# Holding back the third relu and the third square of a visit behind the next product

## The chip, the cores and the metric

The kernel runs on one core of a Trainium2 chip. The metric is the device time of that core in microseconds (us). Runs are told as fast or slow; here a run is slow when it took over 1.5% longer than the fastest of the same kernel. Times are medians of several runs. A ratio is the mean time of one kernel's fast runs over that of the other's fast runs of the same rounds, so it is not quite the ratio of the medians quoted beside it. The engines are called as in the profile: PE is TensorE, PEld its weight loads, ACT ScalarE, DVE VectorE, POOL GpSimd, SP the engine that issues most DMAs.

## The reference

```python
scores = (1 / sqrt(64)) * q @ k.T        # 8 x 12 heads, 448 x 448 each
attn   = maximum(scores, 0) ** 2 / 448
x      = (attn @ v)                      # laid out as 3584 tokens x 768
h      = x @ w_in                        # 768 -> 2048
g      = h * 1 / (1 + exp(-1.702 * h))   # sigmoid form of GELU
out    = g @ w_out                       # 2048 -> 768
```

Inputs and output are float32; the kernel multiplies in float16.

## The kernel before

The 96 heads are handled as 24 units of four heads; a unit has seven score tiles (`s`) and one product with v (`v`). The tokens go through the two weight matrices in eight groups of 384 or 512. The kernel places every instruction by hand: a scheduler of its own emits *visits* (the next three attention items) between *products*, which are `m1` (first matrix, 6 matmuls into `ht`, then a GELU) and `m2` (second matrix, 16 matmuls into `op`, then an evacuation to `osb`). On each engine instructions run in the order of emission.

```python
ps_s = ...tile_pool(name="ps_s", bufs=3, space=PSUM)   # scores and products with v, two banks each
ps_m = ...tile_pool(name="ps_m", bufs=2, space=PSUM)   # ht, op and PE transposes, one bank each

def relu2(u, j, sc):
    ...                                                 # units 3 to 5, j == 3: relu on VectorE
        nc.scalar.activation(out=rl, in_=sc[:, :, 0:S], func=AF.Relu)
    nc.vector.tensor_tensor(out=at, in0=rl, in1=rl, op=ALU.mult)
    return at

def visit(n):
    new = items[pos[0]:pos[0] + n]
    ...
    for t, u, j in new:                                 # first all matmuls of the visit
        if t == "s":
            made.append(scores(u, j))
        else:
            ...                                         # av_mm of all seven ats of the unit
    for (t, u, j), sc in zip(new, made):                # then what reads them
        if t == "s":
            ats[u, j] = relu2(u, j, sc)
        else:
            xt_evac(u)
            done_units[0] = u + 1

def m1(g, f):
    ht = ps_m.tile([128, 512], F32, name="ht", tag="mm")
    ...                                                 # 6 matmuls
    nc.scalar.activation(out=gf[:, 0:n], in_=ht[:, 0:n], func=AF.Gelu_apprx_sigmoid, scale=1.0 / SC)
    nc.gpsimd.tensor_scalar(out=gts[g][:, f, 0:n], in0=gf[:, 0:n], ...)

def m2(g, m, h):
    ...
        op = ps_m.tile([128, 512], F32, name="op", tag="mm")
        ...                                             # 16 matmuls
        nc.vector.tensor_scalar(out=ot[:, lo:lo + w], in0=op[:, 0:w], scalar1=1.0 / SC, ...)
    ...                                                 # store

def step_visit(n):
    visit(n)
    ...
    prefetch(u + 4, u + 2)                              # loads; casts of k (VectorE) and q (GpSimd); DMA transposes
```

A visit's three relus stand in ScalarE's queue ahead of the GELU of the product that follows, and its squares in VectorE's ahead of that product's evacuation.

Of the kernel before, what the change touches and what calls it, by code (L numbers as in the profile page):

```python
# [15 lines left out]
def kernel(  # L16
# [120 lines left out]
    def scores(u, j):  # L137
        st = units[u]
        sc = ps_s.tile([128, 2, 512], F32, name="sc", tag="sc")
        for s in range(2):  # L140
            for a in range(2):
                r = slice(64 * a, 64 * a + 64)
                c = slice(64 * s, 64 * s + 64)
                nc.tensor.matmul(  # L144
                    out=sc[c, a, 0:S],
                    lhsT=st["kT"][r, j, c],
                    rhs=st["qT"][r, :, c],
                    start=True, stop=True)
        return sc

    def relu2(u, j, sc):
        rl = rlp.tile([128, 2, S], F16, name="rl", tag="rl")
        at = atp.tile([128, 2, S], F16, name="at", tag="at")
        if NP <= u < 2 * NP and j == 3:
            nc.vector.tensor_scalar(out=rl, in0=sc[:, :, 0:S], scalar1=0.0, scalar2=None,  # L155
                                    op0=ALU.max)
# [5 lines that stand above are left out]
    def av_mm(u, j, at):  # L162
        st = units[u]
        if j == 0:
            st["av"] = ps_s.tile([128, 2, 512], F32, name="av", tag="sc")
        for s in range(2):
            for a in range(2):
                r = slice(64 * s, 64 * s + 64)
                nc.tensor.matmul(  # L169
                    out=st["av"][64 * a:64 * a + 64, s, 0:S],  # L170
                    lhsT=st["v16"][r, a, 64 * j:64 * j + 64],
                    rhs=at[r, a, :],
                    start=(j == 0), stop=(j == J - 1))
# [3 lines left out]
    def xt_evac(u):  # L177
        b, pr = divmod(u, NP)
        av = units[u]["av"]
        lo = b * J  # L180
        while lo < (b + 1) * J:
            g = max(i for i in range(NG) if gcum[i] <= lo)
            hi = min((b + 1) * J, gcum[g + 1])
            if g not in xts:
                xts[g] = xtp.tile([128, NK, 512], F16, name="xt", tag="xt")
            nc.vector.tensor_copy(  # L186
                out=xts[g][:, 2 * pr:2 * pr + 2, 64 * (lo - gcum[g]):64 * (hi - gcum[g])],
                in_=av[:, :, 64 * (lo - b * J):64 * (hi - b * J)])
            lo = hi
        units[u] = None  # L190
# [12 lines left out]
    ats = {}  # L203
    pos = [0]
    done_units = [0]

    def visit(n):
        new = items[pos[0]:pos[0] + n]
        if new and ("v", new[-1][1], 0) == new[-1] and ("s", new[-1][1], J - 1) in new:
            new.pop()  # L210
        pos[0] += len(new)
        made = []
        for t, u, j in new:
            if t == "s":
                made.append(scores(u, j))
            else:
                for jj in range(J):
                    av_mm(u, jj, ats.pop((u, jj)))
                made.append(None)
        for (t, u, j), sc in zip(new, made):  # L220
            if t == "s":
                ats[u, j] = relu2(u, j, sc)
            else:
                xt_evac(u)
                done_units[0] = u + 1


    gts = {}

    def m1(g, f):  # L230
        n = 64 * gblk[g]
        if f == 0:
            gts[g] = gtp.tile([128, NF, 512], F16, name="gt", tag="gt")
        ht = ps_m.tile([128, 512], F32, name="ht", tag="mm")
        w = win[f // WQ]
        fo = (f % WQ) * 128
        for kk in range(NK):
            nc.tensor.matmul(  # L238
                out=ht[:, 0:n], lhsT=w[:, kk, fo:fo + 128],
                rhs=xts[g][:, kk, 0:n],  # L240
                start=(kk == 0), stop=(kk == NK - 1))
        gf = gfp.tile([128, 512], F32, name="gf", tag="gf")
        nc.scalar.activation(out=gf[:, 0:n], in_=ht[:, 0:n],  # L243
                             func=AF.Gelu_apprx_sigmoid, scale=1.0 / SC)
        nc.gpsimd.tensor_scalar(out=gts[g][:, f, 0:n], in0=gf[:, 0:n],  # L245
                                scalar1=SC, scalar2=1.0, op0=ALU.mult, op1=ALU.mult)

    osb = {}

    def store(g, m, lo, hi, engs):  # L250
        for i in range(2):
            b, j = divmod(gcum[g] + 2 * m + i, J)
            r0 = b * S + j
            engs[i].dma_start(out=out[r0:r0 + 63 * J + 1:J, lo:hi],
                              in_=osb[g, m][64 * i:64 * i + 64, lo:hi])

    def m2(g, m, h):
        if h == 0:
            osb[g, m] = osp.tile([128, DM], F32, name="osb", tag="osb")
        ot = osb[g, m]  # L260
        last = g == NG - 1 and m == gblk[g] // 2 - 1
        for part in range(2 if last and h == 1 else 1):
            w = NOUT // 2 if last and h == 1 else NOUT
            op = ps_m.tile([128, 512], F32, name="op", tag="mm")
            for f in range(NF):
                nc.tensor.matmul(  # L266
                    out=op[:, 0:w],
                    lhsT=gts[g][:, f, m * 128:(m + 1) * 128],
                    rhs=wout[h][f // WO][:, f % WO, part * w:(part + 1) * w],
                    start=(f == 0), stop=(f == NF - 1))  # L270
            lo = h * NOUT + part * w
            nc.vector.tensor_scalar(out=ot[:, lo:lo + w], in0=op[:, 0:w],  # L272
                                    scalar1=1.0 / SC, scalar2=None, op0=ALU.mult)
            if last:
                store(g, m, lo, lo + w, (nc.sync, nc.scalar))
        if h == 1 and not last:
            store(g, m, 0, DM, (nc.sync, nc.sync))

    w_rows = moe_w_in.rearrange("(a kk d) f -> a d kk f", a=2, d=D)

# [31 lines left out]
    with tc.manual_schedule():  # L312
# [23 lines left out]
        while pos[0] < b0:  # L336
            visit(1)
            n += 1
            if n == 4:
                trans_pe(1, "k", 0)  # L340
                trans_pe(1, "q", 0)
                load16(4, "k")
                load16(4, "q")
                load_v(4)
                w1(2)
            if n == 11:
                trans_pe(2, "k", 0)
                trans_pe(2, "q", 0)
                load16(5, "k")
                load16(5, "q")  # L350
                load_v(5)
            if n == 19:
                trans_pe(3, "k", 0)
                trans_pe(3, "q", 0)
                w1(3)
        visit(3)


# [3 lines left out]
        for f in range(NF):  # L362
            m1(0, f)
            if f in (2, 8):
                trans_pe(4 + f // 8, "k", 0)
                trans_pe(4 + f // 8, "q", 0)
            if f in pool_work:
                pool_work[f]()
            if f % 2 == 1 or f > 12:
                visit(min(3, b1 - pos[0]))  # L370
# [19 lines left out]
        for m in range(gblk[0] // 2):  # L390
            m2(0, m, 0)
# [18 lines left out]
        for n, (it, tv) in enumerate(moe):  # L410
            if n == 0:
                prefetch(9, 7)
            if n == 2:
                prefetch(9, 8)
                acc = 2.0
            if it[0] == "m1":
                g = it[1]
                need = NP * min(B, -(-gcum[g + 1] // J))
                while done_units[0] < need:
                    step_visit(3)  # L420
                m1(*it[1:])
                acc += t1(g)
                if it[2] == NF - 1:
                    m1_done = g + 1
            else:
                m2(*it[1:])
                acc += T2
            while acc >= tv and pos[0] < len(items):

                if all(t == "s" or u // NP - 2 < m1_done for t, u, j in items[pos[0]:pos[0] + 3]):  # L430
                    step_visit(3)
                    acc -= tv
                else:
                    acc = tv - 0.01
# [30 lines left out]
```

## Time and profile before

The kernel took 413.97 us (three runs, 412.87 to 414.67). The profiled execution spans 410.5 us.

| stretch, us | what runs | PE busy | ACT busy | DVE busy |
|---|---|---|---|---|
| 0 to 60 | attention of units 0 to 5, first `ht` | 43.8 of 60 | 41.7 | 38.4 |
| 60 to 105 | first `op`, units 6 to 8 | 42.9 of 45 | 26.2 | 22.7 |
| 105 to 335 | all three kinds mixed, units 9 to 23 | 224.3 of 230 | 125.3 | 118.5 |
| from 335 | `ht` and `op` alone | 71.3 of 76 | 12.5 | 10.2 |

To read it: PE is nearly full from 60 us on, so an idle ACT or DVE costs nothing there; only a gap on PE does.

### The profile page before, as it was taken

The page shows a single profiled execution, that of the slowest core. Times are in us where ns is not written, and L with a number is a line of the kernel's source. Part 1 is how long each engine was busy: PE and PEld are TensorE (multiplying, and loading weights), DVE is VectorE, ACT ScalarE, POOL GpSimd, SP SyncE. Part 2 cuts the span into 40 slices and gives each one's busy share as a digit, 9 for nine tenths or more (in the row PEclk, how much of TensorE's full clock was granted, in tenths as well). Part 3 has the DMA queues.
Part 4 walks back from the last instruction along what each step waited for, and adds up shares of the span by engine and source line. Part 5 has one row for each costly group of instructions (what it writes and reads, how often), then busy time and mean ns, then how long its engine had stood idle before and what let it go on. Part 6 is the DMA issues. An engine that isn't in the chain of part 4 may idle for free.

```text
span 410.5 us, 7828 instructions
## 1 busy us (share of the span) xinstructions
PE 382.3 (93%) x3192; PEld 200.7 (49%) x3192; DVE 189.7 (46%) x294; ACT 205.7 (50%) x297; POOL 131.6 (32%) x200
## 2 busy tenths in 40 slices
PE   3777999999998999999999898999999999999995
PEld 2433445444444554454455454444445556455564
DVE  0995773367665464366466445546354421110121
ACT  3984770776664555456655635547645511222100
POOL 8443433453433142333233223312312211223100
PEclk9999999999999999999999999999999999999999
DMA  8999996889668654963667465845121111111123
GB/s 123 196 205 204 205 301 127 188 187 225 153 150 182 162 102 81 235 123 101 170 112 155 80 154 152 195 53 75 43 46 40 38 40 39 40 38 41 38 77 79
DMA packets 65222, 50.85 MB, mean 124 GB/s; under 512 B 35745, under 2 KB 61729, under 8 KB 65185
## 3 DMA queue, kind: packets, MB, share of 16 engines
q1 hardware_dynamic: 47792, 35.60, 35.5%
q0 software_dynamic: 17152, 14.55, 23.8%
q8 instruction: 25, 0.41, 0.4%
q10 hardware_dynamic: 240, 0.20, 0.2%
q14 instruction: 13, 0.10, 0.1%
HBM read 45.61 MB, written 11.01 MB: 138 GB/s over the span
## 4 chain that ended last, share of the span: by engine, by line
PE 76%; ACT 9%; DVE 8%; issue 4%; DMA 2%; POOL 0%; ACTq 0%; DVEq 0%; POOLq 0%
PE op L266 35%; PE ht L238 27%; ACT rl L158 7%; PE av L169 7%; PE sc L144 6%; DVE at L159 4%; ACT gf L243 2%; DMA q<-in_q_dram 1%; DVE rl L155 1%; DMA qT<-q 1%; DVE xt L186 1%; DVE kT L134 1%; DVE qT L134 0%; DVE osb L272 0%; POOL gt L245 0%
## 5 line engine op out<-in xcount | busy, mean ns | idle before, releaser
L158 ACT ACTIVATE rl<-sc 128x896 f16<-128x896 f32 x165 | 140.9, 920 | 58.9 <-PE sc L144 58.9
L238 PE MATMUL ht<-xt,win 128*128 128x384 f16 (+1 forms) x768 | 158.8, 353 | 4.6 <-DVE kT L134 2.1
L266 PE MATMUL op<-wout,gt 128*128 128x384 f16 (+1 forms) x912 | 153.2, 323 | 4.1 <-ACT gf L243 4.1
L245 POOL TENSOR_SCALAR gt<-gf 128x384 f16<-128x384 f32 (+1 forms) x128 | 78.4, 612 | 239.3 <-ACT gf L243 237.5
L159 DVE TENSOR_TENSOR at<-rl 128x896 f16<-128x896 f16 x168 | 113.3, 687 | 78.4 <-ACT rl L158 78.2
L243 ACT ACTIVATE gf<-ht 128x384 f32<-128x384 f32 (+1 forms) x128 | 69.1, 553 | 113.5 <-PE ht L238 100.1
L266 PEld LDWEIGHTS <-gt 128*128 128x128 f16 x912 | 88.0, 98 | 66.1 <-issue 8.8
L238 PEld LDWEIGHTS <-win 128*128 128x128 f16 x768 | 71.0, 98 | 82.7 <-issue 22.9
L272 DVE TENSOR_SCALAR osb<-op 128x384 f32<-128x384 f32 (+1 forms) x57 | 31.2, 548 | 121.2 <-PE op L266 121.2
L144 PE MATMUL sc<-qT,kT 64*64 64x448 f16 x672 | 47.5, 363 | 6.9 <-DVE qT L134 3.6
L169 PE MATMUL av<-at,v 64*64 64x448 f16 x672 | 36.5, 351 | 1.9 <-ACT rl L158 1.5
L144 PEld LDWEIGHTS <-kT 64*64 64x64 f16 x672 | 16.7, 106 | 32.2 <-issue 20.7
L186 DVE CAST xt<-av 128x768 f16<-128x768 f32 (+2 forms) x36 | 26.8, 772 | 8.8 <-PE av L169 8.8
L169 PEld LDWEIGHTS <-v 64*64 64x64 f16 x672 | 19.5, 107 | 15.7 <-issue 6.4
L88 POOL DMA_DIRECT2D v<-in_v_dram x24 | 17.9, 747 | 3.9 <-DMA win<-in_moe_w_in_dram 2.2
L101 POOL CAST q<-qst 128x896 f16<-128x896 f32 x18 | 16.9, 941 | 0.3
L101 DVE CAST k<-kst 128x896 f16<-128x896 f32 x18 | 14.0, 784 | 0.0
L127 PE MATMUL tr<-ident,k 128*64 128x128 f16 x84 | 4.2, 253 | 5.2 <-DMA k<-in_k_dram 5.2
L134 DVE COPY qT<-tr 128x896 f16<-128x896 f16 (+1 forms) x6 | 3.4, 570 | 7.5 <-ACT qT L132 7.5
L127 PEld LDWEIGHTS <-k 128*64 128x64 f16 x84 | 3.1, 128 | 6.9 <-DMA k<-in_k_dram 5.2
L283 POOL DMA_DIRECT2D win<-in_moe_w_in_dram x8 | 5.4, 682 | 3.0 <-DMA k<-in_k_dram 1.7
L127 PE MATMUL tr<-ident,q 128*64 128x128 f16 x84 | 4.2, 251 | 1.3 <-ACT gf L243 0.7
(17 smaller groups left out, 26.3 us busy)
## 6 DMA issues: line engine op xcount, KB each, us to landing
out_dram<-osb SPq DMA_DIRECT2D x54, 192.0 KB, 2.7
kst<-in_k_dram SPq DMA_DIRECT2D x18, 448.0 KB, 5.0
qst<-in_q_dram SPq DMA_DIRECT2D x18, 448.0 KB, 5.7
v<-in_v_dram POOLq DMA_DIRECT2D x24, 224.0 KB, 4.6
win<-in_moe_w_in_dram POOLq DMA_DIRECT2D x8, 384.0 KB, 11.4
wout<-in_moe_w_out_dram POOLq DMA_DIRECT2D x4, 768.0 KB, 12.0
k<-in_k_dram POOLq DMA_DIRECT2D x6, 224.0 KB, 8.8
q<-in_q_dram POOLq DMA_DIRECT2D x6, 224.0 KB, 8.7
```

What stands on the lines that cost most here:

```text
L88: nc.gpsimd.dma_start(out=x, in_=quad(v, b, pr))
L101: eng.tensor_copy(out=o, in_=i)
L144: nc.tensor.matmul(out=sc[c, a, 0:S], lhsT=st["kT"][r, j, c], rhs=st["qT"][r, :, c], start=True, stop=True)
L158: nc.scalar.activation(out=rl, in_=sc[:, :, 0:S], func=AF.Relu)
L159: nc.vector.tensor_tensor(out=at, in0=rl, in1=rl, op=ALU.mult)
L169: nc.tensor.matmul(out=st["av"][64 * a:64 * a + 64, s, 0:S], lhsT=st["v16"][r, a, 64 * j:64 * j + 64], rhs=at[r, a, :], start=(j == 0), st ...
L186: nc.vector.tensor_copy(out=xts[g][:, 2 * pr:2 * pr + 2, 64 * (lo - gcum[g]):64 * (hi - gcum[g])], in_=av[:, :, 64 * (lo - b * J):64 * (hi ...
L238: nc.tensor.matmul(out=ht[:, 0:n], lhsT=w[:, kk, fo:fo + 128], rhs=xts[g][:, kk, 0:n], start=(kk == 0), stop=(kk == NK - 1))
L243: nc.scalar.activation(out=gf[:, 0:n], in_=ht[:, 0:n], func=AF.Gelu_apprx_sigmoid, scale=1.0 / SC)
L245: nc.gpsimd.tensor_scalar(out=gts[g][:, f, 0:n], in0=gf[:, 0:n], scalar1=SC, scalar2=1.0, op0=ALU.mult, op1=ALU.mult)
L266: nc.tensor.matmul(out=op[:, 0:w], lhsT=gts[g][:, f, m * 128:(m + 1) * 128], rhs=wout[h][f // WO][:, f % WO, part * w:(part + 1) * w], sta ...
L272: nc.vector.tensor_scalar(out=ot[:, lo:lo + w], in0=op[:, 0:w], scalar1=1.0 / SC, scalar2=None, op0=ALU.mult)
```

## The change

The third relu of a visit is to let the GELU of the next product pass, so that the PSUM buffer (PSUM is where the matmuls put their results) of that product comes free sooner; and the third square is to let the evacuation of an `op` pass, for the same purpose.

```diff
+    held = []
+
+    def release():
+        while held:
+            u, j, sc = held.pop()
+            ats[u, j] = relu2(u, j, sc)
+
     def visit(n):
         ...
         pos[0] += len(new)
+        release()
         ...
-        for (t, u, j), sc in zip(new, made):
-            if t == "s":
-                ats[u, j] = relu2(u, j, sc)
-            else:
+
+        for i, ((t, u, j), sc) in enumerate(zip(new, made)):
+            if t == "v":
                 xt_evac(u)
                 done_units[0] = u + 1
+            elif i == 2:
+                held.append((u, j, sc))
+            else:
+                ats[u, j] = relu2(u, j, sc)
     def m1(g, f):
         ...                                             # after the GELU and its scaling
+        release()
     def m2(g, m, h):
         ...                                             # after the evacuation and the store
+        release()
```

## The prediction

> **What bounds the kernel now.** I began with the page: busy shares first, then the groups of instructions.
>
> ```profile
> PE 382.3 (93%) x3192; PEld 200.7 (49%) x3192; DVE 189.7 (46%) x294; ACT 205.7 (50%) x297; POOL 131.6 (32%) x200
> ...
> L158 ACT ACTIVATE rl<-sc 128x896 f16<-128x896 f32 x165 | 140.9, 920 | 58.9 <-PE sc L144 58.9
> ```
>
> TensorE (PE) is busy for 93% of the span, ScalarE (ACT) and VectorE (DVE) for about half. Matmul ends are modelled, so I measured the distance from one matmul's start to the next instead. Inside one product it is steady: 0.1625 us for 384 columns, 0.216 us for 512. A product of the first matrix (`ht`, 6 matmuls) takes 0.98 or 1.30 us, one of the second (`op`, 16 matmuls) 2.60 us, the three scores of a visit 0.69 us. From 330 us on there is no gap at all. The distances that exceed these sum to some 25 us, 13.4 us of them before 50 us, where ACT feeds the attention alone. So PE is the bound from about 30 us on, and a change to ACT and DVE order can win only the rest, about 11 us of gaps. The list of waits names who ends the gaps:
>
> ```profile
> ACT gf L243 <- PE ht L238: 100.1, 57, 8.6
> ...
> PE op L266 <- ACT gf L243: 4.1, 7, 0.6
> ```
>
> The first row is idleness of an engine that is not the bound, and costs nothing. The second is the target: seven times a product `op` waited for a GELU (`gf`). The timeline of PE, ACT and DVE around one of them:
>
> ```profile
> 111.27 0.76 PE L144 MATMUL sc<-qT,kT 64*64 64x448 f16 x12
> ...
> 111.71 2.54 ACT L158 ACTIVATE rl<-sc 128x896 f16<-128x896 f32 x3 [2.27 <-PE sc L144]
> ...
> 111.96 2.12 PE L238 MATMUL ht<-xt,win 128*128 128x384 f16 x12
> ...
> 114.11 0.89 ACT L243 ACTIVATE gf<-ht 128x384 f32<-128x384 f32 x2
> ...
> 114.67 2.76 PE L266 MATMUL op<-wout,gt 128*128 128x384 f16 x16 [0.58 <-ACT gf L243]
> ```
>
> The visit's scores start at 111.27. ACT takes the three relus from 111.71, 0.80 us apart, and reaches the GELU only at 114.11, although the first `ht` was ready long before. The next `op` reuses that `ht`'s PSUM buffer (the pool `ps_m` has two), and starts at 114.67. The 12 matmuls of the two `ht` take 12 x 0.1625 = 1.95 us, so it could have started at 111.96 + 1.95 = 113.91. The loss is 0.75 us, more than the 0.58 us printed as idle, because a modelled matmul end covers the rest. The same gap of 0.75 us stands at 113.8, 157.5, 229.0, 235.1, 247.7, 253.8 and 320.4: each is a visit of three scores, then two 384-column `ht`, then an `op`.
>
> A second kind of gap is on DVE, near 131 us:
>
> ```profile
> 131.10 0.61 DVE L101 CAST k<-kst 128x896 f16<-128x896 f32 x1
> ...
> 131.64 0.54 DVE L272 TENSOR_SCALAR osb<-op 128x384 f32<-128x384 f32 x1
> ...
> 132.23 1.14 PE L238 MATMUL ht<-xt,win 128*128 128x384 f16 x6 [1.19 <-DVE osb L272]
> ```
>
> There the visit is followed by `op` and then two `ht`; a k cast and the third square stand ahead of the evacuation of `op` (`osb`), and the second `ht` waits for it. Its loss is 1.36 us from start to start.
>
> **What the Trainium skill says.** "PSUM — Partial Sum Buffer", section "Engine vs sequencer instructions", says that the queues of ScalarE and VectorE are strict FIFO; the trace agrees, the GELU at 114.11 comes after all three relus. "ScalarE: Activation LUTs", section "What ACT_TABLE_LOAD costs", gives 186 ns + 0.833 ns per element, less about 93 ns back to back: 932 ns for 896 elements against 920 ns measured, and 839 ns spacing against 0.80 us here. "Perfetto Trace Analysis", section "Optimization Strategy", says that a repeating bubble on the engine that should be saturated can mean too few buffers; seven equal gaps at a two-buffer pool are that. "SBUF — State Buffer", section "SBUF: two separate sides", says that a VectorE operation with two SBUF inputs and a GpSimd operation lock each other out; I see one square of 2.02 us at 128.09 beside a GpSimd cast, against 0.61 us for its neighbours, which fits.
>
> **The change part by part.** No instruction is added or removed. The order of ACT changes where a product `ht` follows a visit whose third item is a score: relu, relu, GELU, relu. Where `op` follows, ACT keeps its order and DVE gets square, square, evacuation, square. Visits of fewer than three items, or whose third item is the product with v, keep theirs. The k cast issued right after a visit moves ahead of the held square.
>
> *Gains.* (1) The GELU moves up by one relu slot, 0.80 us, to 111.71 + 2 x 0.80 = 113.31. From its start to the `op` start took 114.67 - 114.11 = 0.56 us, so `op` is free at 113.87, just before 113.91. Seven gaps: 7 x 0.75 = 5.25 us. (2) Two visits followed by three 512-column `ht` (164.2 and 293.3 us) lose 0.217 us each the same way: 0.43 us. (3) Evacuations move up by one square slot, 0.53 us: the gap at 130.7 us falls by 0.53, that of 0.46 us at 299.5 us vanishes: 0.99 us together. (4) At 93.0 us scores wait 0.79 us for a DMA transpose of k, whose cast stood behind a third square; the cast moves up by about 0.8 us: 0.73 us. Sum 7.4 us.
>
> *Losses.* The held relu now waits for the `ht` and for its GELU. From the start of `ht` to the start of its GELU on a free ACT is 1.24 us (132.23 to 133.47) or, with 512 columns, 1.56 us (164.62 to 166.17); the next relu follows 0.39 or 0.48 us later and takes 0.92 us. So after a visit of three scores it ends 3.4 or 3.65 us after the first score instead of 2.97. It holds a score buffer (three in `ps_s`) until then. That is harmless where two or more products separate visits, which is nearly everywhere after 96 us; it hurts where one `ht` does:
>
> ```profile
> 76.01 0.76 PE L144 MATMUL sc<-qT,kT 64*64 64x448 f16 x12 [0.64 <-DMA qT<-q]
> ...
> 76.44 2.53 ACT L158 ACTIVATE rl<-sc 128x896 f16<-128x896 f32 x3 [0.38 <-PE sc L144]
> ...
> 76.70 1.47 PE L238 MATMUL ht<-xt,win 128*128 128x512 f16 x6
> ...
> 78.10 0.57 PE L144 MATMUL sc<-qT,kT 64*64 64x448 f16 x8
> ...
> 78.85 0.62 ACT L243 ACTIVATE gf<-ht 128x512 f32<-128x512 f32 x1
> ...
> 79.02 0.38 PE L144 MATMUL sc<-qT,kT 64*64 64x448 f16 x4 [0.35 <-ACT rl L158]
> ```
>
> The third score of the second visit waits for the relu of the third score of the first. It could start at 76.01 + 3.65 + 0.05 = 79.71 instead of 79.02: 0.69 us. A like place at 86 us costs about 0.08 us, and one at 45 us, two narrow `ht` apart, 0.16 us. At 59 to 61 us the product with v needs the square of the held relu: the GELU can begin at 59.29, the relu at 59.69, its square ends at 61.28 instead of 60.87: 0.41 us. And in the transposes of q and k on PE:
>
> ```profile
> 46.21 1.73 ACT L158 ACTIVATE rl<-sc 128x896 f16<-128x896 f32 x2
> ...
> 47.82 0.50 ACT L243 ACTIVATE gf<-ht 128x384 f32<-128x384 f32 x1
> 48.37 0.58 PE L127 MATMUL tr<-ident,q 128*64 128x128 f16 x14 [0.43 <-ACT gf L243]
> ...
> 48.76 0.61 DVE L134 COPY kT<-tr 128x896 f16<-128x896 f16 x1
> ...
> 49.43 0.81 PE L238 MATMUL ht<-xt,win 128*128 128x384 f16 x4 [0.48 <-DVE kT L134]
> ```
>
> The GELU can start at 46.28 + 1.24 = 47.52, which lets the q transpose begin 0.3 us sooner. But the held relu then runs 47.92 to 48.84, its square to 49.5, and the copy of kT stands behind that square on DVE: 49.42 to 50.03 instead of 48.76 to 49.37, and the `ht` behind it starts 0.66 us later. The twin place at 35 us is bound by a relu on DVE and stays. Sum of losses 0.16 + 0.66 + 0.41 + 0.69 + 0.08 = 2.0 us.
>
> Net 7.4 - 2.0 = 5.4 us, and 413.97 - 5.4 = 408.6 us, 1.3% faster.
>
> **The rivals.** *ACT becomes a wait of its own*: PE catches up with held relus in more places than those five. For it: wherever two 512-column `ht` separate two visits I find only 0.08 us of slack (third score at 3.78 us, buffer free at 3.70). Against it: those are few, and ACT is half idle. Five such places missing by 0.3 us would take back 1.5 us: 410 us. *Early losses spread*: they delay casts and transposes, and DMA waits at 75 and 93 us grow instead of shrinking; then only (1) to (3) less the losses remain, 6.7 - 2.0 = 4.7 us, or 3.9 us if the wait at 93 us doubles: 409.3 to 410.1 us. *DMA and GpSimd hide it all*: work moved in time meets other lockouts on DVE; for it, the 1.36 us gap is such an accident; against it, the seven target gaps have no transfer in their path. That would give 412 us. *More than I count*: if the losses before 75 us vanish in the DMA wait there (0.71 us), and all of the 1.36 us goes, 408.6 - 0.71 - 0.83 = 407.1 us.
>
> **Range and chances.** The gain is an ordering effect of which 5.7 us is direct to see, and the losses are timed by hand to some 0.3 us each, with unseen ones more likely than unseen gains. I choose 408.6 us, range 406.3 to 411.8. The three runs before spread by 1.8 us. Faster by over 2% needs 8.3 us, more than all gains without losses: 4%. Slower by over 2% would need many new waits: 1%. Within 2%: 95%.
>
> **What would show it right or wrong.** Right: the wait of `op` for `gf` falls from 4.1 us to under 0.5; ACT shows two relus, GELU, relu after visits; the `ht` at 132 waits about 0.5 us less; the stage from 105 to 335 us shortens by 6 to 7 us and the first 105 us lengthen by 1 to 2. New rows appear for scores or products with v waiting for a relu near 79 and 61 us and for `ht` waiting for kT near 50 us. Wrong: the seven gaps stay partly, because the GELU waits for something but its place in the queue; or new waits of scores for relus appear in the long stage; or the transposes land later for the visits.

## The result, and the profile after

The changed kernel took 407.9 us (four runs, 407.53 to 408.25) against 413.42 us of the kernel before in the same rounds: ratio 0.9863, 95% interval 0.9834 to 0.9891. That is faster by 1.4%, within the 2% called the same. Later, beside the other versions, it took 409.01 us (six runs, 407.48 to 409.95) against 413.15 us: ratio 0.9889 (0.9864 to 0.9913). The profiled execution spans 406.5 us.

The page of the changed kernel, engines and the group of `op`; the number after the last bar is PE's idle time just before such matmuls:

```profile
PE 383.3 (94%) x3192; PEld 202.2 (50%) x3192; DVE 190.7 (47%) x294; ACT 205.3 (51%) x297; POOL 130.8 (32%) x200
...
L278 PE MATMUL op<-wout,gt 128*128 128x384 f16 (+1 forms) x912 | 153.2, 323 | 0.0
```

ACT and DVE do the same work as before. The idle time ahead of `op`, 4.1 us before, is zero. Its list of waits has no row of `op` waiting for a GELU any more, and these two rows grew (2.1 and 1.1 us before):

```profile
PE ht L249 <- DVE kT L134: 3.4, 2, 1.8
...
PE sc L144 <- ACT rl L158: 1.8, 4, 1.1
```

So the loss moved in part to a copy of kT and to score buffers. The stage from 105 to 335 us shows the net. Columns are the stretch, its length, and busy time with the number of instructions of PE, PEld, DVE, ACT, POOL, then PE clock, DMA share and GB/s; first before, then after:

```profile
105.00:335.00 230.00, 224.30 (x1859) 115.30 (x1858) 118.46 (x176) 125.31 (x182) 68.39 (x102) 1.00 0.53 114
```

```profile
105.00:335.00 230.00, 229.34 (x1905) 119.41 (x1897) 120.92 (x179) 128.24 (x187) 71.14 (x106) 1.00 0.53 118
```

PE went from 224.3 to 229.3 us busy of 230, and got through 46 matmuls more. The timeline of the changed kernel at the first of the seven places, the one that the prediction shows at 111.27 us:

```profile
113.88 0.76 PE L144 MATMUL sc<-qT,kT 64*64 64x448 f16 x12
...
114.31 1.73 ACT L158 ACTIVATE rl<-sc 128x896 f16<-128x896 f32 x2 [1.46 <-PE sc L144]
...
114.57 2.12 PE L249 MATMUL ht<-xt,win 128*128 128x384 f16 x12
...
115.92 0.50 ACT L254 ACTIVATE gf<-ht 128x384 f32<-128x384 f32 x1
...
116.30 0.94 ACT L158 ACTIVATE rl<-sc 128x896 f16<-128x896 f32 x1
...
116.53 2.76 PE L278 MATMUL op<-wout,gt 128*128 128x384 f16 x16
```

Two relus, GELU, relu, as the diff says. The GELU starts 2.04 us after the first score instead of 2.84, so 0.80 earlier, and `op` starts 1.96 us after the first `ht`, which is the length of two `ht`: no gap is left. The second kind of gap, on DVE, in the changed kernel:

```profile
132.43 0.61 DVE L101 CAST k<-kst 128x896 f16<-128x896 f32 x1
132.96 0.55 DVE L284 TENSOR_SCALAR osb<-op 128x384 f32<-128x384 f32 x1
...
133.43 0.61 DVE L159 TENSOR_TENSOR at<-rl 128x896 f16<-128x896 f16 x1
133.56 1.14 PE L249 MATMUL ht<-xt,win 128*128 128x384 f16 x6 [0.66 <-DVE osb L284]
```

The evacuation (L284) now precedes the third square, and the `ht` waits 0.66 us by this view where it waited 1.19. The k cast is still ahead. Where one `ht` separates two visits, the changed kernel pays:

```profile
77.81 0.76 PE L144 MATMUL sc<-qT,kT 64*64 64x448 f16 x12 [0.63 <-DMA qT<-q]
...
80.07 0.60 ACT L254 ACTIVATE gf<-ht 128x512 f32<-128x512 f32 x1
80.57 2.53 ACT L158 ACTIVATE rl<-sc 128x896 f16<-128x896 f32 x3
...
81.53 0.38 PE L144 MATMUL sc<-qT,kT 64*64 64x448 f16 x4 [1.05 <-ACT rl L158]
```

The GELU at 80.07 stands ahead of the held relu in the group at 80.57, and the third score of the second visit starts at 81.53, 3.72 us after the first visit's first score; before it was 3.01.

The PE order of both kernels is the same, 3192 matmuls. I paired the k-th of one trace with the k-th of the other and looked where the distance between them jumps. Apart from the first 38 us, it stays constant to 0.06 us except at a few places. All but the last of them are terms of the prediction's sum:

| place in the trace before, us | foreseen, us | measured jump, us |
|---|---|---|
| seven gaps of `op` (113.8 to 320.4) | -5.25 | 7 x -0.75 = -5.25 |
| third of three `ht` (164.2, 293.3) | -0.43 | 2 x -0.22 |
| evacuations (130.7, 299.5) | -0.99 | -0.53 - 0.46 = -0.99 |
| DMA transposes (93.0) | -0.73 | -0.26; 0.0 in the repeated run |
| score buffer (45.8) | +0.16 | +0.14 |
| transposes on PE, kT copy (47.7 and 48.7) | +0.66 | -0.30 + 1.08 = +0.78 |
| product with v (60.1) | +0.41 | +0.38 |
| score buffers (78.3 and 86.8) | +0.69 + 0.08 | +0.70 + 0.09 |
| product with v (95.5) | none | +0.25; 0.0 in the repeated run |

They sum to -4.59 us. The two profiles differ by 4.04, because this profile of the changed kernel also has a window of 3.4 us from 27.5 us at half PE clock, which pushed PE back by some 0.75 us net, and chance differences of -0.25 us at the start.

The last row belongs to the change. The k cast now stands ahead of the held square, and by the trace that square (97.18 to 98.20 us, 1.03 us long instead of 0.61, beside a GpSimd operation) ends just before the last matmuls of the product with v start, at 98.25. What was won at the transposes was so lost 1.5 us later. The version below that moves only the GELU has -0.61 us at the transposes and +0.61 here, and shows it as a wait:

```profile
95.57 1.03 DVE L101 CAST k<-kst 128x896 f16<-128x896 f32 x1
...
96.52 2.09 DVE L159 TENSOR_TENSOR at<-rl 128x896 f16<-128x896 f16 x3
...
97.59 0.38 PE L169 MATMUL av<-at,v 64*64 64x448 f16 x4 [0.41 <-DVE at L159]
```

### The profile page after: what moved, and what is told of

It reads as the page before. It is cut to its first block, busy times and chain, and to the rows that moved or that the text cites. A ratio compares the mean times of both kernels' runs of the same rounds, so it can differ in the third digit from the quotient of the medians.

```text
span 406.5 us, 7792 instructions
## 1 busy us (share of the span) xinstructions
PE 383.3 (94%) x3192; PEld 202.2 (50%) x3192; DVE 190.7 (47%) x294; ACT 205.3 (51%) x297; POOL 130.8 (32%) x200
## 4 chain that ended last, share of the span: by engine, by line
PE 84%; DVE 6%; ACT 5%; issue 2%; DMA 2%; POOL 0%; ACTq 0%; DVEq 0%; POOLq 0%
PE op L278 35%; PE ht L249 33%; PE sc L144 7%; PE av L169 7%; ACT rl L158 4%; DVE at L159 3%; DMA q<-in_q_dram 1%; DVE rl L155 1%; DVE xt L186 1%; DMA qT<-q 1%; ACT gf L254 1%; DVE kT L134 1%; DVE k L101 0%; POOL gt L256 0%; PE tr L127 0%
## 5 line engine op out<-in xcount | busy, mean ns | idle before, releaser
L158 ACT ACTIVATE rl<-sc 128x896 f16<-128x896 f32 x165 | 144.8, 920 | 49.7 <-PE sc L144 49.7
L159 DVE TENSOR_TENSOR at<-rl 128x896 f16<-128x896 f16 x168 | 114.9, 692 | 87.7 <-ACT rl L158 87.4
L254 ACT ACTIVATE gf<-ht 128x384 f32<-128x384 f32 (+1 forms) x128 | 70.4, 550 | 119.6 <-PE ht L249 106.8
L284 DVE TENSOR_SCALAR osb<-op 128x384 f32<-128x384 f32 (+1 forms) x57 | 31.3, 549 | 108.0 <-PE op L278 106.5
L144 PE MATMUL sc<-qT,kT 64*64 64x448 f16 x672 | 48.6, 367 | 6.8 <-DVE qT L134 3.0
L169 PE MATMUL av<-at,v 64*64 64x448 f16 x672 | 38.0, 360 | 2.3 <-ACT rl L158 1.4
L116 POOL DMA_DIRECT2D q<-in_q_dram x6 | 4.3, 713 | 3.0 <-PE sc L144 1.3
```

Source lines behind the costliest of these rows:

```text
L144: nc.tensor.matmul(out=sc[c, a, 0:S], lhsT=st["kT"][r, j, c], rhs=st["qT"][r, :, c], start=True, stop=True)
L169: nc.tensor.matmul(out=st["av"][64 * a:64 * a + 64, s, 0:S], lhsT=st["v16"][r, a, 64 * j:64 * j + 64], rhs=at[r, a, :], start=(j == 0), st ...
```

## The experiments

All versions gave correct results. "Jump" below is the same pairing of matmuls against the profile of the kernel before; single jumps repeat to 0.01 us from profile to profile, save those at 93.0 and 95.5 us, while whole spans do not, so causes are read from jumps.

**Only the GELU's part.** The relu is held only where `m1` comes next:

```diff
-            elif i == 2:
+            elif i == 2 and hold[0]:
-        def step_visit(n):
+        def step_visit(n, nxt):                          # nxt: kind of the next product
+            hold[0] = nxt == "m1"
```

> The third relu is held only where a product of the first matrix (ht) follows the visit; where op follows, the order of before stays. Theory (queue place of the GELU is worth 5.25 + 0.43 us in nine gaps, queue place of the evacuation on VectorE 0.99 us in two): all nine gaps behind a GELU stay closed, the gaps of 1.36 us near 131 us and of 0.46 us near 299 us of the kernel before come back, so about 1.0 us slower than the changed kernel: 408.9 us, 4.5 us faster than before. Rival (most of the gain comes from the evacuations on VectorE): 411 us or more.

409.46 us (six runs) against 413.07; ratio 0.9909 (0.9884 to 0.9935). Jumps: -0.75 at all seven places, -0.22 at both others, none at 130.7 and 299.5, and the five early losses as in the table (+0.14, +0.78, +0.38, +0.70, +0.09). The GELU's place is worth 5.7 us by jumps; the median is 0.6 us off what was expected, within what medians scatter here.

**Only the evacuation's part**, the same with `"m2"`:

> The third relu is held only where op follows the visit, so no GELU moves. Theory: the seven gaps of 0.75 us and the two of 0.22 us are all there, the two on VectorE shrink by 0.53 and 0.46 us, none of the early losses occurs: about 1.0 us faster than before, 412.4 us. Rival (evacuations carry most of the gain): 409 us or less.

412.33 us (six runs) against 413.07; ratio 0.998 (0.9954 to 1.0006), not resolved from none by time. The jumps resolve it: -0.53 and -0.46 at the two evacuations, none at the nine GELU places, no early losses. At 93.0 us there is one of +0.95, a longer wait for a DMA transpose. The list of waits of this version still has the full row of the kernel before:

```profile
PE op L279 <- ACT gf L255: 4.1, 7, 0.6
```

So the rival that gives the evacuations most of the gain falls.

**Hold only where nothing is lost.** `hold[0] = items[pos[0]][1] >= 9`, off before:

> The third relu is held only from attention unit 9 on, that is after the stretch in which a single ht separates two visits or a transpose follows. Theory (the changed kernel pays about 2 us before 100 us, for held relus in front of a kT copy, of the product with v and of a score buffer, and wins all of the rest later): none of the losses at 49, 61 and 80 us, all late gaps closed, 406.0 us, some 2 us faster than the changed kernel (406.7 if the 0.3 to 0.7 us won at the DMA wait near 93 us is lost with it). Rival (the losses are absorbed by the DMA waits that follow at 75 and 93 us): same time as the changed kernel, 407.9 us.

406.35 us (six runs) against 413.07; ratio 0.9835 (0.981 to 0.986). All late jumps are as before (-0.75 seven times, -0.22 twice, -0.54 and -0.46), and the five early ones are gone. By jumps, 2.09 us of loss are undone. At 93.0 us there is a jump of +0.26 instead of -0.26. So the losses of the change are real, are not absorbed by the DMA waits after them, and were avoidable.

**Hold two relus.** `elif i >= 1`, released in order:

> The second and the third relu of a visit are held, so the GELU moves up by two slots, 1.6 us. Theory (one slot is already just enough for op, 113.87 against 113.91 us by hand, so a second slot wins nothing, and each held relu keeps its score buffer longer): the nine gaps are as closed as with one held, scores wait for relus in more places, among them the visits that two 512-column ht separate, and the early losses about double: about 412 us, 4 us slower than the changed kernel. Rival (the more is moved behind the GELU the better, as ScalarE is half idle): 407.9 us or less.

418.19 us (six runs) against 413.07; ratio 1.0121 (1.0096 to 1.0147): slower than the kernel before. The nine gaps are as closed as with one (-0.75, -0.22), and the evacuation at 130.7 has its full gain (-1.07). But where two 512-column `ht` separate two visits, the third score now waits; a place near 197 us in this version:

```profile
195.32 1.72 ACT L158 ACTIVATE rl<-sc 128x896 f16<-128x896 f32 x2
...
197.09 0.38 PE L144 MATMUL sc<-qT,kT 64*64 64x448 f16 x4 [0.43 <-ACT rl L158]
```

The second held relu reads its buffer in the group at 195.32, and the third score of the next visit starts at 197.09, with 0.43 us of idle shown and 0.73 us lost from start to start. There are six such places (4.4 us), and the early ones grew: +1.75 us at the kT copy, 2.3 us before the product with v, 1.5 us at 78 us. The direction was right; the size, 4 us over the changed kernel, was less than half of the 10 us that came; the expectation gives no sum. The hand slack of 0.08 us with one held relu fits: one more relu slot of 0.80 us, less 0.08, is 0.72 us, against 0.73 lost.

**Take the relu away instead of moving it.** The kernel before, with the third relu of a three-score visit on VectorE, ahead of the squares, from unit 6 on:

```diff
+        if len(new) == 3 and all(t == "s" for t, u, j in new) and new[0][1] >= 2 * NP:
+            rl3 = rlp.tile([128, 2, S], F16, name="rl", tag="rl")
+            nc.vector.tensor_scalar(out=rl3, in0=made[2][:, :, 0:S], scalar1=0.0,
+                                    scalar2=None, op0=ALU.max)
         ...                                             # relu2 then only squares rl3
```

> The kernel before, nothing held, but from unit 6 on the third relu of a visit of three scores runs on VectorE, ahead of the visit's squares. The GELU gets the same slot on ScalarE as in the changed kernel, by taking the relu away instead of moving it. Theory (the nine gaps are ScalarE's queue ahead of the GELU and nothing else): all nine closed, 5.7 us; the score wait of 0.52 us near 79 us goes too, since the buffer is read earlier; the evacuation near 131 us comes some 0.5 to 1 us later behind one more VectorE operation: 407.4 us. Rival (the gaps close for another reason that comes with holding, such as the later square or score buffer): the nine gaps stay, 412 us or more.

406.91 us (five runs) against 412.96; ratio 0.9859 (0.9837 to 0.9882). All nine gaps closed by the same amounts with nothing held, and the 0.52 us at 78.3 went. The evacuation at 130.7 did not get later, as I had feared; its gap stayed. So what kept `op` waiting is ScalarE's queue ahead of the GELU, whichever way it is shortened.

**The fourth gain, tested alone.** The late-only version, but in early visits loads and casts go ahead of the third relu and square:

```diff
+            late = items[pos[0]][1] >= 9
+            hold[0] = True
             visit(n)
             ...
             prefetch(u + 4, u + 2)
+            if not late:
+                release()
```

> As the late-only version, but before unit 9 the loads and casts for later units are issued ahead of the visit's third relu and square, with no hold across a product. Theory of the prediction's gain (4) (scores near 94 us wait for a transpose whose cast stood behind a third square): the cast is about 0.6 us earlier and the gap of about 1.05 us there in the late-only run falls by 0.5 to 0.7 us: 405.8 us. Rival (the transpose is late because of the transfers, not because of its cast): no change, 406.4 us.

406.37 us (five runs) against 412.96; ratio 0.9841 (0.9818 to 0.9864): as late-only. The jump at 93.0 is +0.23 against +0.26. The timelines of late-only and of this version around it, VectorE's k cast, SP's transposes, PE's scores:

```profile
87.99 0.62 DVE L101 CAST k<-kst 128x896 f16<-128x896 f32 x1
...
90.04 2.37 SPq L108 DMA_TRANSPOSE qT<-q  x1
...
95.50 0.57 PE L144 MATMUL sc<-qT,kT 64*64 64x448 f16 x8 [0.98 <-DMA qT<-q]
```

```profile
86.99 0.62 DVE L101 CAST k<-kst 128x896 f16<-128x896 f32 x1
...
89.08 3.10 SPq L108 DMA_TRANSPOSE qT<-q  x1
...
95.28 0.57 PE L144 MATMUL sc<-qT,kT 64*64 64x448 f16 x8 [0.95 <-DMA qT<-q]
```

Paired with the scores before them (87.89 and 87.70), the cast is 0.81 us earlier. But the second transpose then occupied its issue for 3.10 us instead of 2.37 and ended at 92.18 against 92.41, and the scores waited for it as long (0.95 and 0.98 us). Both views name the transpose of q as what the scores waited for, while my step went by that of k, which is issued ahead of it. In both versions q's own cast, on GpSimd, was over (at 85.96 and 85.77 us) more than 3 us before its transpose was issued. So the wait ends with the landing of q's transpose, and does not follow the k cast. Over all fourteen profiles it ran from 0.0 to 1.7 us, with 0.44 us between two profiles of one and the same version. What holds up that transpose was not found.

**Casts behind the product, late.** From unit 9 on, what `prefetch` emits comes after the next product:

```diff
+                if late:
+                    owed.append(lambda: prefetch(u + 4, u + 2))   # run at the start of release()
+                else:
+                    prefetch(u + 4, u + 2)
```

> As the late-only version, but from unit 9 on the loads and casts for later units are issued behind the product that follows the visit. Theory (what is left of the gap near 131 us, 0.83 us, is the k cast of 0.53 us ahead of the evacuation): the gap falls to 0.3 us and nothing else changes: 405.8 us. Rival (later casts make the transposes late for their visits): new waits of scores for a transfer, 407 us or more.

405.33 us (five runs) against 412.96; ratio 0.9816 (0.9792 to 0.9839). The jump at 130.7 is -1.07 instead of -0.53, and no new wait appeared. Around it:

```profile
128.85 2.40 PE L253 MATMUL ht<-xt,win 128*128 128x384 f16 x12
129.52 0.54 DVE L288 TENSOR_SCALAR osb<-op 128x384 f32<-128x384 f32 x1
129.99 0.61 DVE L101 CAST k<-kst 128x896 f16<-128x896 f32 x1
...
130.52 0.61 DVE L159 TENSOR_TENSOR at<-rl 128x896 f16<-128x896 f16 x1
```

Evacuation, cast, square; the two `ht` run on as one group of 12 and their rest is a gap of 0.29 us. The cast was the rest of the second gap.

**Both cast moves.**

> The changes of the two runs before together. Theory: their gains add, 405.3 us. Rival: as told there.

406.76 us (six runs, 404.52 to 409.24) against 412.96; ratio 0.9858 (0.9827 to 0.9888). Its profile has all the jumps of the run before; the spread of the runs left the addition undecided, so it was repeated.

**Repeats, and a last version.** The changed kernel and the two versions above ran again in one call, with one more: casts behind the product and late hold, and in units 6 to 8 the third relu on VectorE first.

> The changed kernel again, unchanged, in the same call as the versions that seem to beat it: 407.9 us, 1.4% faster than before.

> The version that holds late and puts the casts behind the product, again: 405.4 us, some 2.5 us faster than the changed kernel beside it. If it is no faster than that kernel here, the difference lay between the calls.

> The version with both cast moves again, whose six runs spread over 4.7 us: 405.4 us, as the one beside it, since its first half won nothing at the gap near 94 us; if it is again at 406.5 us or more with a wide spread, something in it is unstable.

> Late hold and casts behind the product, and in units 6 to 8 the third relu of a visit of three scores on VectorE first. Theory: the score wait near 79 us (0.52 us in the kernel before, there again in the late-only versions) goes, as it went with the relu on VectorE everywhere: 404.9 us. Rival (what is won there is lost at the transfer some 15 us later): 405.4 us.

| version | median, us | lowest to highest | ratio to before, 95% interval |
|---|---|---|---|
| changed kernel | 409.01 | 407.48 to 409.95 | 0.9889 (0.9864 to 0.9913) |
| casts behind, late hold (five fast runs) | 406.99 | 404.81 to 407.77 | 0.9839 (0.9814 to 0.9865) |
| with early casts first | 405.48 | 405.00 to 405.89 | 0.9814 (0.9793 to 0.9834) |
| casts behind, late hold, early relu on VectorE | 404.85 | 404.37 to 407.31 | 0.9807 (0.9784 to 0.9831) |

The sixth run of the second row, 411.48 us, was slow. This time the other of the two spread, so the spread belongs to neither, and early casts add nothing that can be told from scatter. The last version has the -0.52 us at 78.3 and the late jumps; it is 1.9% faster than the kernel before and the best median of all. Its lead over the two above it is inside their scatter; its lead over the changed kernel, 4.2 us by medians with no overlap of the runs, is not. Part of those 4.2 us is the clock, as told next: among runs with a granted clock of 0.999 or more the lead is 2.9 us (407.5 against 404.6).

Where the scatter comes from shows in part. Six of the fourteen profiles, the changed kernel's own among them, have one or two windows of 3.41 us, between 15 and 55 us, in which the granted PE clock (the share of full speed that PE was allowed) is 0.5 and the spacing of matmuls doubles (from 0.16 to 0.32 us for 384 columns). The profile of the first repeat in the table has one at 38.4 us: the distance to the kernel before jumps by some 1.5 us in it, where PE is full. That of the second has two. The kernel before shows none in its one profile. In three more profiles (late-only, the repeat of both cast moves, the last version) the first record of full clock stands at 17.7 to 18.3 us, against 11.7 to 14.5 in the others, and PE falls back by 1.0 to 1.3 us before it. The times agree: in the repeat of the changed kernel, the three runs with a granted clock of 0.992 to 0.994 took 409.5 to 410.0 us, the three at 0.999 or more 407.5 to 408.5.

## Why the prediction was right

The time foreseen was 408.6 us and the change came to 407.9 and, in the repeat, 409.0. That the gain foreseen, 5.4 us, is so near the first measured one, 5.5, is in part luck: the repeat gave 4.1 us, and the jumps sum to 4.6. By jumps the part after 105 us is 6.7 us shorter, within the 6 to 7 foreseen; the miss lies before it.

- *PE bounds, and a two-slot PSUM pool makes it wait for the GELU*: shown. Moving the GELU up by one slot (the change), and freeing the slot (relu on VectorE), close the same nine gaps by the same amounts; moving it by two wins nothing more there.
- *The slack of `op` after the move, 113.87 against 113.91*: it suffices. `op` follows without a gap at all seven places; its size, 0.04 us, was not measured.
- *Evacuations*: shown, to 0.01 us, and separately in the evacuation-only version.
- *"At 93.0 us scores wait 0.79 us for a DMA transpose of k, whose cast stood behind a third square; the cast moves up by about 0.8 us: 0.73 us"*: this step failed. I had taken the cast of k for what sets the landing. In the kernel before, k's transpose had landed at 93.2 us and q's only at 94.0, just before the scores started at 94.13. The early-cast version moved the k cast by 0.81 us and the wait did not follow. In the changed kernel the wait fell by 0.26 and 0.0 us, and the 0.26 was lost again at the product with v, which waits for the square of the held relu: of 0.73 us nothing was won.
- *Losses*: the terms listed are shown, 2.09 us against 2.0; the product with v at 95.5 us was missed. The kT term was 0.78 instead of 0.66: in the trace the square ahead of the held one took 0.93 us instead of 0.61 (48.81 to 49.74 us), so the held square and the copy of kT began about 0.1 us later than reckoned.
- *Rival, ACT becomes a wait of its own*: not with one held relu, beyond the places foreseen; it is what happens with two.
- *Rival, early losses spread into the DMA waits*, and its opposite, *absorbed by them*: neither. Late-only undoes them nearly in full.
- *Rival, DMA and GpSimd hide it all*: no; the jumps at the nine gaps are the same in every profile that closes them. The lockout read into the square at 128.09 us was tested by no run, and the cast beside it began 0.58 us later, at 128.67. *More than I count*: no; the gap of 1.36 us kept 0.83 us, as its k cast stayed ahead.
- *That unseen losses are likelier than unseen gains*: the gain near 93 us that did not come was the one such term, and half clock windows another that I had not thought of; together they are some 1.5 us in the first profile.

## What to carry to other kernels

When a saturated engine shows the same gap several times, find the buffer it waits for and count what stands ahead of its reader in that reader's queue: here one operation moved behind the reader closed it, and a second one only added waits. An operation that is held keeps its own input buffer and delays whatever is emitted behind it, so hold it only in the stretches where more than one product lies before the next use. To attribute such small terms, pair the k-th instruction of the bound engine in both traces and read where their distance jumps; that resolves 0.1 us where medians scatter by 1 to 2.

## What the Trainium skill lacked or had wrong

- "TensorE: Matmul & The Clock Gate", Part 1, has the half clock as the state of an idle or cold array, left after a busy window of about 3.4 us, and tells of kernels in which waits or short idle spells bring it back. Here eight windows of 3.41 us at 0.5 came in the middle of work, in six of fourteen profiles between 15 and 55 us. PE had been busy for 46 to 62% of the 3.41 us before each, yet 51% from 12.6 us in the kernel before brought none; how sparse the work must be, the page does not say. By its formula (Terms: the time at reduced clock times one minus the granted share) a window costs 1.7 us as an estimate; 0.7 to 1.5 us were lost in each here.
- "ScalarE: Activation LUTs", section "What ACT_TABLE_LOAD costs", gives an overlap of about 93 ns for back-to-back operations. Relus of 0.92 us started 0.80 us apart here, an overlap of 0.12 us (the prediction's 932 and 839 ns are estimates from the formula of that section); a relu after a GELU of 0.49 us started 0.39 us after it, 0.10 us.
- No page that I read says how long an issued DMA transpose may take under load. The same transpose of q held its issue for 1.27 to 3.10 us in the fourteen profiles, and scores waited for it between 0.0 and 1.7 us; in the two profiles of the changed kernel it was 2.36 and 3.02 us.
- "Perfetto Trace Analysis", section "Optimization Strategy", names buffer shortage for consistent bubbles, and otherwise advises to make the dependencies start sooner. Here the shortage was cured at an unchanged number of buffers, by the order in the queue of the engine that empties them: seven gaps of 0.75 us went. The section does not link the two.
